# Decode attention with cached keys: in 13 of 16 heads the turned keys stream past the queries

## The chip, the cores and the metric

The kernel runs on one core of one Trainium2 chip. The metric is the device time of one execution in microseconds. TensorE is called PE here, VectorE DVE, ScalarE ACT, GpSimd POOL, and SyncE, which issues nearly all DMAs, SP.

## The reference

Eight sequences decode one token each (x is 8 x 1 x 448). The same attention block and the same mixer block are applied twice, in turn:

```python
x = x + _A_ref(_layernorm(x), A_k_cache, A_v_cache, A_wq, A_wo)
x = x + _B_ref(_layernorm(x), B_w1, B_w2, B_w3, B_w4)
x = x + _A_ref(_layernorm(x), A_k_cache, A_v_cache, A_wq, A_wo)
x = x + _B_ref(_layernorm(x), B_w1, B_w2, B_w3, B_w4)

def _A_ref(x, k_cache, v_cache, wq, wo):        # Hq 16, Hkv 8, Sk 4096, Dh 256
    q = (x @ wq).reshape(B, Sq, Hq, Dh).transpose(0, 2, 1, 3)
    k, v = repeat of the caches: two query heads share one key/value head
    scores = einsum("bhqd,bhkd->bhqk", q, k) * Dh ** -0.5
    return (softmax(scores) @ v).reshape(B, Sq, Hq * Dh) @ wo
```

With one token per sequence the token mixer of `_B_ref` sees only shifted, padded positions, so that the block is, in effect, a layernorm, a layernorm again, and a gelu MLP (448 to 1792 to 448) with its residual. Everything is bfloat16. Keys and values of one batch row and one key head are 2 MB each, and there are 64 such pairs. Since the caches are used by both attentions, they would be read twice; the kernel keeps a part of them in SBUF between the two.

## The kernel before, in words

**Units and slots.** A "head" here is one batch row and one key head, with its two query columns, in one of the two layers (attentions): 8 rows x 8 heads x 2 layers = 128. Its 4096 keys are loaded with 32 consecutive keys per partition, and are cut into four quarters (`u`) of eight key blocks (`s`) each. SBUF has 30 quarter slots of 4 KB per partition, shared by keys and values (`kv`). A load (`issue_kv`, L636) takes one to four quarters into neighbouring slots and waits on SP until the slots' last readers are done.

**One head's front (`front`, L1084).** For each quarter two pieces of 4 blocks are turned on PE: keys come as pairs of bfloat16 seen as one float32, so that a 128 x 128 float32 transpose turns 256 head dimensions at once (`transpose_piece`, L1401). Each piece fills one of four PSUM banks `psT`, and is copied back into its slot by DVE or ACT, whichever the planner picks (`evacuate`, L1332 and L1333). Even and odd head dimensions then lie interleaved along a slot's columns. The scores (`score`, L1119) use each turned block as the stationary operand, once for the even and once for the odd dimensions (`c`), and stream the two query columns, repeated 24 times (`REP`), past it: 64 matmuls of 48 columns per head. The 64 columns of scores lie in `psM` from column 64 (`SB`). They are copied to `sS` (L1177), reduced to a maximum (DVE, then POOL), and exponentiated on ACT into `pT` (L1194).

**One head's back (`back`).** P.V runs in four column strips of the array (32 matmuls of 256 columns, L1228), is copied out as two bfloat16 parts (`oS`, L1242 and L1244), summed over the strips (L1252), scaled (`oT`, L1258), and multiplied by the rows of wo (L1278) into a running row in `psR`. After the seventh head of a layer the row is turned back to columns by way of `oW` (L1291, L1293, L1060), and the eighth head is added.

**Order.** Key heads 0, 1 and 2 are "free" heads, loaded in both layers. Heads 3 to 6 keep their turned keys in SBUF from the first attention to the second; head 7 keeps one quarter, and leaves two quarters in the four `psT` banks and one half quarter in `kh`. Some values are kept too (`KEPT_V`). Per batch row the order is: first attention of the heads 3 to 7, with the free heads of the next row scored ahead; the MLP (`mid`, `mlp`), while the values of the next row's free heads pass; second attention in the order 6, 7, 5, 4, 3, 0, 1, 2. The second attention's queries are computed one head ahead (`second_queries`, L878 on PE, L1452 on DVE, into `q2T`). The results of the first six rows go through their last MLP together beside row 5.

A planner in the kernel (`Plan.schedule`) lays out all operations as a list schedule with written durations and priorities. It fixes each engine's order and each slot's tenant, lets "ev" operations go to DVE or ACT, and inserts filler matmuls (L1604) into PE's gaps. On the chip each engine goes through its list in that order and waits on semaphores.

Of the kernel before, what the change touches and what calls it, by code (L numbers as in the profile page):

```python
# [6 lines left out]
P = 128  # L7
B = 8
D = 448
HKV = 8  # L10
DH = 256
F = 1792
NC5 = 5
# [33 lines left out]
PV0 = 0  # L47
# [4 lines left out]
ST = 504  # L52
Q1 = 176


# [29 lines left out]
class Plan:  # L85
# [69 lines left out]
    def schedule(self):  # L155
# [78 lines left out]
        while n < len(self.ops):  # L234
# [128 lines left out]
            o.end = end  # L363
            if o.frees is not None:
                self.free_at[o.frees.slot] = end + self.LAT[e]
                self.tenant[o.frees.slot] = o
            for s in o.succ:
# [104 lines left out]
def bass_interleave_layers__gqa_block_cached__mixer_s_mlp__decode_kernel(  # L472
# [67 lines left out]
    rsy = sb("rsy", [P, 2, B], f32)  # L540
    q1b = [sb(f"q1b{i}", [P, 32], bf) for i in range(2)]
    lin = sb("lin", [P, 2, 2], f32)
    kh = sb("kh", [P, 1024], bf)
    q2T = [sb(f"q2T{i}", [P, 32], bf) for i in range(2)]
    cursor[0] = (cursor[0] + 31) // 32 * 32
# [13 lines left out]
    oW = over("oW", [P, 2, 2 * P], bf, hb)  # L559
    o_row = over("o_row", [B, D], bf, hb)  # L560
    cursor[0] = max(cursor[0], hb0 + 8 * P)
# [11 lines left out]

    sS = [sb(f"sS{i}", [P, 64], f32) for i in range(NS)]
    oS = sb("oS", [P, 2, DH], bf)
# [78 lines left out]
    YB = ["yb"]  # L654
    REG = ["hb", "g1", "hT", "t_h", "xc", "yb"]

    def const_a(gp):
        gp.memset(ident_f[:, :], 0.0)
        gp.memset(x_row[:, D:D + P], 0.0)
        gp.memset(mask[:, :], 1.0)  # L660
        gp.memset(x3T[:, :, :], 0.0)
        for t, one, minus in [(t, 1, 2) for t in x1c + x2c] + [(xf, 1, 0), (xf, 4, 5)]:
            gp.memset(t[:, :, one:one + 1], 1.0)
            last = gp.memset(t[:, :, minus:minus + 1], -1.0)
        return last
    plan.op("pool", const_a, 1.0, "const", wr=["ident0", "xr2", "mask0", "one", "x3all"])

# [150 lines left out]
    def norm(src, skey, second, B):  # L818
# [13 lines left out]
        mark(pe(mm, 36, rd=[skey, "one"], wr=[key], banks=[bk]))  # L832
        mo, xcv = mom[:, 0:2, 0:B], xc[:, :, 0:B]
        dv(lambda v: v.tensor_single_scalar(mo, ps[:, 0:2 * B].rearrange("p (c n) -> p c n", n=B),
# [7 lines left out]
        if second:  # L842
# [3 lines left out]
        dv(lambda v: v.tensor_tensor(xcv, src, bcast(mom[:, 0, 0:B], NC5, 1), ALU.add),  # L846
           rd=["mom", skey], wr=["xc", "g1"])
        dv(lambda v: v.tensor_tensor(xcv, xcv, bcast(mask[:, :], B, 2), ALU.mult), rd=["xc", "mask"],
           wr=["xc"])
        dv(lambda v: v.tensor_tensor(yb[:, :, 0:B], xcv, bcast(rsy[:, c - 1, 0:B], NC5, 1), ALU.mult),  # L850
           rd=["xc", "rsy"], wr=["yb", "g1"])
        if second:

            bs = base[:, :, 0:B]
            dv(lambda v: v.tensor_tensor(bs, xcv, bcast(rsy[:, 0, 0:B], NC5, 1), ALU.mult),
               rd=["xc", "rsy"], wr=["base"])
            dv(lambda v: v.tensor_tensor(bs, bs, src, ALU.add), rd=["base", skey], wr=["base"])
# [105 lines left out]
    def mlp(src, skey, n, dst, dkeys, rows_open=False):  # L963
# [5 lines left out]
        m = 14 * n  # L969
        h_, a_ = hb[:, 0:m], g1[:, 0:m]  # L970
        def scaled(r, y, keys):
# [28 lines left out]
        else:  # L1000
            norm(src, skey, True, n)
            pe(lambda t: h_mms(t, lambda kc: yb[:, kc, 0:n], ch, 0, n, n), 56,
               rd=YB + W3, wr=[kb], banks=[bk])
            dv(lambda v: v.tensor_copy(h_, ch[:, 0:m]), rd=[kb], wr=["hb"], banks=[bk])

        HB = ["hb"] + [("hb", r) for r in range(1, n) if few]
        dv(lambda v: v.scalar_tensor_tensor(a_, h_, GELU_C * GELU_K, h_, ALU.mult, ALU.mult),
           rd=HB, wr=["g1", "xc", "yb"])
        dv(lambda v: v.scalar_tensor_tensor(a_, a_, GELU_K, h_, ALU.add, ALU.mult),
           rd=HB + ["g1"], wr=["g1"])  # L1010
        plan.op("act", lambda a: a.activation(a_, a_, ACT.Tanh), 0.3, "chain",
                rd=["g1"], wr=["g1"], prio=urge[0] + len(plan.ops))
        if few and dst is not None:
# [5 lines left out]
               rd=["base", ("y", 0, B - 2), skey], wr=["base"])  # L1019
        dv(lambda v: v.scalar_tensor_tensor(hT[:, 0:m], a_, 1.0, h_, ALU.add, ALU.mult),  # L1020
           rd=HB + ["g1"], wr=["hT"])

# [4 lines left out]
        def y_mm(t, mts):  # L1027
            last = None
            for mt in mts:
                for fc in range(14):  # L1030
                    r = hT[:, fc * n:(fc + 1) * n]
                    if not few:
                        last = dup(t, ch, yc + mt * yw, yw, w4_sb, fc * D, mt, r, fc == 0, fc == 13)
                        continue
                    a = fc * D + (mt * P if mt < 4 else D - P)
                    if mt == 3 and fc == 13:
                        last = dup(t, ch, yc + mt * yw, yw, w4_sb, fc * D, mt, bcast(r, yw, 1), False, True)
                        continue
                    last = t.matmul(ch[:, yc + mt * yw:yc + (mt + 1) * yw], w4_sb[:, a:a + P], bcast(r, yw, 1),
                                    start=(fc == 0), stop=(fc == 13), skip_group_check=(mt == 3))  # L1040
            return last
        parts = Y_PARTS if few else [range(NC5)]
        for mts in parts:
            pe(lambda t, mts=mts: y_mm(t, mts), 14 * len(mts), rd=["hT"] + W4, wr=[kb], banks=[bk], width=yw)
        ps4 = ch[:, yc:yc + NC5 * yw].rearrange("p (a n) -> p a n", n=yw)[:, :, 0:n]
# [32 lines left out]
    def first_q(b, prio):  # L1078
        for c in range(2):
            dv(lambda v, c=c: v.tensor_copy(  # L1080
                q1b[b % 2][:, :].rearrange("p (h c j) -> p h c j", c=2, j=2)[:, :, c, :],
                psM[:, Q1 + b:Q1 + 32 * B:B].rearrange("p (h j c) -> p h c j", j=2, c=2)[:, :, c, :]),
               rd=["q1"], wr=[("q1b", b % 2, c)], banks=[M], prio=prio)

    def front(layer, b, h, prio=None):
# [8 lines left out]
        if layer == 0:  # L1094
            def rhs(c):
                return q1b[b % 2][:, 4 * h + 2 * c:4 * h + 2 * c + 2]
            qk = [("q1b", b % 2, 0), ("q1b", b % 2, 1)]
        else:
            def rhs(c):
                return q2T[b % 2][:, 4 * h + 2 * c:4 * h + 2 * c + 2]  # L1100
            qk = [("q2", b, h)]
        ks = dict(kept_k)
# [21 lines left out]
        def score_op(u, ss, where_of, keys):  # L1124
# [3 lines left out]
                           rd=qk + keys, wr=[("sc", par, x) for x in range(u, 4)], banks=[bk],  # L1128
                           prio=prio and prio + len(plan.ops))
        for u in range(4):  # L1130
            full = [("s", ks[u], 0), ("s", ks[u], 1)]
# [14 lines left out]
            if last_head and u == 1:  # L1146
                if layer == 0:
                    score_op(u, range(4), of_kh, ["kh"])
                    o = score_op(u, range(4, 8), of, [("s", ks[u], 1, 0), ("s", ks[u], 1, 1)])
                    o.frees = ks[u]  # L1150
                else:
# [3 lines left out]
                continue  # L1155
            if layer and last_head and u in (2, 3):
                pass
            o = score_op(u, range(8), of, full)
            if layer and h == first2[b] and u == 3:
# [9 lines left out]
            if layer and u == 3 and h == first2[b]:  # L1169
                lent[b] = ks[u]  # L1170
            elif u not in keep_k:
                o.frees = ks[u]
        hi = len(plan.ops) - 10 ** 5
# [30 lines left out]
    def back(layer, b, h):  # L1204

        kept_k, vs, held, nr = state.pop((layer, b, h))
        free_p.append(nr)
        keep_v = KEPT_V.get(h, ()) if layer == 0 else ()
# [12 lines left out]
        for u in range(4):  # L1221

            def pv(t, u=u, q=vs[u]):
                last = None
                for s in range(8):
                    i = 8 * u + s
                    g4 = 32 * (i % 4)
                    last = t.matmul(ps[g4:g4 + 2, PV0:PV0 + DH], pT[nr][:, i, :],  # L1228
                                    slot_ap(q, s * 256, 256), start=(i < 4), stop=(i >= 28),
# [8 lines left out]
            if u not in keep_v:  # L1238
                o.frees = vs[u]

# [84 lines left out]
    tcount = [0]  # L1325
    held_banks = set()

    def evacuate(i, pc, bank):
# [84 lines left out]
    def result(n, at):  # L1413
# [3 lines left out]
        def ot(t):  # L1417
            last = None
            for kc in range(4):
# [5 lines left out]
        mark(dv(lambda v: v.tensor_copy(o_row[0:n, :], ps[0:n, :].bitcast(bf)[:, 0:D]), dur=0.5,  # L1425
           rd=[key], wr=["o_row"] + REG, banks=[bk]))
        plan.op("sp", lambda eng: eng.dma_start(out[at:at + n, 0, :], o_row[0:n, :]), 0.1, "out",
                rd=["o_row"] + REG, wr=[("done", n)],
                dma=(s_out, 16), prio=loads[0] + OUT_AT)
# [17 lines left out]
    def second_queries(b, h, prio):  # L1447
# [4 lines left out]
        dv(lambda v: v.scalar_tensor_tensor(  # L1452
            q[:, 4 * h:4 * h + 4].rearrange("p (c j) -> p c j", c=2),
            cs_q[:, 4 * h:4 * h + 4].rearrange("p (c j) -> p c j", c=2), mom2[b % 2][:, 2:3],
            psM[:, SC:SC + 4].rearrange("p (j c) -> p c j", c=2), ALU.mult, ALU.add),
           rd=["psM", ("mom2", b), "cs_q"], wr=[("q2", b, h)], banks=[M], prio=prio)

# [206 lines left out]
```

## Time and profile before

| what | value |
|---|---|
| median of three runs | 1105.56 us (1102.48, 1105.56, 1107.56) |
| span of the profiled execution | 1108.6 us, 42701 instructions |
| mean granted clock of TensorE | 0.918 |
| PE busy, matmuls | 964.7 us, 19483 |
| DVE busy, ACT busy | 587.9 us, 291.6 us |
| HBM read | 434.18 MB, 392 GB/s over the span |
| packets of q1, share of 16 DMA engines | 61268, 96.6% |

The span is that of the one profiled execution, from its first to its last instruction. No time of its own is reported for that execution beside the span; the span is 1.0 us above the slowest of the three runs and 3.0 us above their median. "busy" counts instructions as the profiler shows them; a matmul's row holds its way through the pipeline too, so that the mean of one (285 ns for a transpose) is longer than the distance from one to the next. "issue" as a releaser means that an engine waited for nothing that the profile shows.

### The profile page before, as it was taken

To read this page: it belongs to the slowest core of one execution; us is meant where nothing else is said; L and a number is where in the kernel's file an instruction comes from. 1 tells how busy PE (TensorE), PEld (TensorE's weight loads), DVE (VectorE), ACT (ScalarE), POOL (GpSimd) and SP (SyncE) were. 2 spreads that over 40 slices of the span, in tenths; PEclk is the share of its full clock that TensorE was granted. 3 is DMA by queue.
4 is the path that set the end of the run, shared out by engine and by line. 5 is a ranking of instruction groups with operands and counts; after the bars stand their busy time and mean duration, and the time that the engine had idled before them with its cause. 6 is when DMAs were issued, how large, how long until landed. Compare 5 with 4: busy or idle time off the path is not lost.

```text
span 1108.6 us, 42701 instructions
## 1 busy us (share of the span) xinstructions
PE 964.7 (87%) x19483; PEld 772.7 (70%) x19483; DVE 587.9 (53%) x1869; ACT 291.6 (26%) x862; POOL 98.2 (9%) x277
## 2 busy tenths in 40 slices
PE   4889889898899888898989988899889998888885
PEld 4678657785678756697668855788567885786673
DVE  4245445565465553565546554566546665455644
ACT  1133112340234311243124411244023330233230
POOL 0000010110100001010000101011010100110010
PEclk9899989997999888999799988999789998999796
DMA  9999999999999999999999999999999999999892
GB/s 334 409 425 417 380 406 425 422 419 388 397 423 426 399 388 406 410 399 407 377 425 425 421 394 400 425 422 416 388 398 426 422 372 377 397 420 383 292 415 91
DMA packets 61456, 436.95 MB, mean 394 GB/s; under 512 B 6606, under 2 KB 9820, under 8 KB 40924
## 3 DMA queue, kind: packets, MB, share of 16 engines
q1 hardware_dynamic: 61268, 434.22, 96.6%
q8 instruction: 153, 2.51, 0.9%
q14 instruction: 27, 0.22, 0.0%
q10 hardware_dynamic: 8, 0.00, 0.0%
HBM read 434.18 MB, written 0.01 MB: 392 GB/s over the span
## 4 chain that ended last, share of the span: by engine, by line
PE 58%; DMA 25%; SPq 5%; DVE 5%; issue 4%; ACT 2%; POOL 1%; DVEq 0%
PE psT L1401 22%; PE psM L1119 16%; DMA kv<-in_A_v_cache_dram 13%; DMA kv<-in_A_k_cache_dram 11%; PE psP L1228 10%; SPq L636 4%; PE psR L1278 4%; PE psM L878 2%; SPq L619 1%; ACT pT L1194 1%; PE psP L1252 1%; DVE oS L1244 1%; DVE oS L1242 1%; DMA w_sb<-in_B_w_dram 1%; PE psM L1060 1%
## 5 line engine op out<-in xcount | busy, mean ns | idle before, releaser
L1401 PE MATMUL psT<-ident_f,kv 128*128 128x128 f32 x2752 | 384.4, 285 | 14.7 <-DMA kv<-in_A_k_cache_dram 14.0
L1332 DVE COPY kv<-psT 128x512 f32<-128x512 f32 x411 | 282.5, 691 | 158.8 <-PE psT L1401 155.5
L1401 PEld LDWEIGHTS psT<-ident_f,kv 128*128 128x128 f32 x2752 | 307.8, 145 | 38.4 <-issue 18.9
L1333 ACT COPY kv<-psT 128x512 f32<-128x512 f32 x309 | 180.6, 587 | 456.9 <-PE psT L1401 368.1
L1228 PE MATMUL psP<-kv,pT 128*2 128x256 bf16 x4096 | 190.6, 295 | 39.0 <-issue 21.2
L1119 PEld LDWEIGHTS psM<-q2T,kv 128*128 128x128 bf16 x3968 | 124.6, 100 | 48.0 <-issue 36.5
L1119 PE MATMUL psM<-q2T,kv 128*128 128x48 bf16 x3968 | 139.4, 188 | 17.1 <-issue 15.7
L1119 PEld LDWEIGHTS psM<-q1b,kv 128*128 128x128 bf16 x4032 | 131.4, 97 | 19.2 <-issue 8.5
L1119 PE MATMUL psM<-q1b,kv 128*128 128x48 bf16 x4032 | 140.0, 184 | 4.9 <-ACT pT L1194 2.6
L1228 PEld LDWEIGHTS psP<-kv,pT 128*2 128x2 bf16 x4096 | 76.5, 83 | 79.6 <-issue 33.9
L1184 POOL PARTITION_ALL_REDUCE gm<-pm x128 | 45.6, 357 | 767.0 <-DVE pm L1182 694.9
L1194 ACT ACTIVATE pT<-sS,nb,fac 128x32 bf16<-128x32 f32 x128 | 52.9, 419 | 158.7 <-DVE nb L1188 158.7
L1177 DVE COPY sS<-psM 128x64 f32<-128x64 f32 x128 | 28.6, 224 | 117.3 <-PE psM L1119 114.9
L1242 DVE CAST oS<-psP 128x256 bf16<-128x256 f32 x128 | 54.0, 422 | 68.0 <-PE psP L1228 66.6
L1278 PE MATMUL psR<-wo_sb,oT 128*1 128x448 bf16 x444 | 68.8, 396 | 3.5 <-DVE oT L1258 2.3
L1198 POOL PARTITION_ALL_REDUCE Db<-rs x128 | 51.3, 400 | 208.4 <-ACT pT L1194 208.4
L1194 ACT ACTIVATE pT<-sS,nb 128x32 bf16<-128x32 f32 x128 | 40.9, 327 | 72.1 <-DVE nb L1188 72.1
L1252 PEld LDWEIGHTS psP<-sel,oS 128*128 128x128 bf16 x512 | 25.4, 100 | 49.1 <-DVE oS L1244 42.9
L1252 PE MATMUL psP<-sel,oS 128*128 128x2 bf16 x512 | 32.3, 167 | 31.3 <-DVE oS L1244 29.3
L1244 DVE TENSOR_TENSOR oS<-psP,oS 128x256 bf16<-128x256 f32 x128 | 54.2, 423 | 3.4
L878 PEld LDWEIGHTS psM<-x2c,wq_sb 128*128 128x128 bf16 x768 | 30.8, 99 | 16.6 <-DVE pm L1182 6.6
L1258 DVE TENSOR_TENSOR oT<-psP,rc 128x4 bf16<-128x4 f32 x128 | 20.3, 159 | 37.2 <-PE psP L1252 34.3
(187 smaller groups left out, 652.4 us busy)
## 6 DMA issues: line engine op xcount, KB each, us to landing
kv<-in_A_k_cache_dram SPq DMA_DIRECT2D x66, 2048.0 KB, 18.8
kv<-in_A_v_cache_dram SPq DMA_DIRECT2D x53, 2048.0 KB, 16.0
kv<-in_A_v_cache_dram SPq DMA_DIRECT2D x196, 512.0 KB, 8.1
kv<-in_A_k_cache_dram SPq DMA_DIRECT2D x43, 512.0 KB, 8.1
kv<-in_A_k_cache_dram SPq DMA_DIRECT2D x13, 1536.0 KB, 15.1
kv<-in_A_v_cache_dram SPq DMA_DIRECT2D x15, 1024.0 KB, 9.5
kv<-in_A_v_cache_dram SPq DMA_DIRECT2D x6, 1536.0 KB, 10.7
wo_sb<-in_A_wo_dram SPq DMA_DIRECT2D x1, 3584.0 KB, 45.6
```

Of the source, the lines that this page charges most:

```text
L878: last = t.matmul(bank[:, at + i * step:at + i * step + copies], w, r, start=(kc == 0), stop=(kc == 3))
L1119: last = t.matmul(ps[:, SB + 2 * i:SB + 2 * i + 2 * REP], a()[:, c:256:2], bcast(rhs(c), REP, 1), start=(c == 0), stop=(c == 1))
L1194: return a.activation(pT[nr][:, :, :].rearrange("p i j -> p j i")[:, jj, :], sview[:, jj, :], ACT.Exp, bias=nb[nm][:, jj:jj + 1], scale=sc ...
L1198: plan.op("pool", lambda gp: gp.partition_all_reduce(Db[nr][:, :], rs[nr][:, :], P, RO.add), 0.5, "sum", rd=[("rs", nr, 0), ("rs", nr, 1)] ...
L1228: last = t.matmul(ps[g4:g4 + 2, PV0:PV0 + DH], pT[nr][:, i, :], slot_ap(q, s * 256, 256), start=(i < 4), stop=(i >= 28), skip_group_check= ...
L1242: plan.op("dve", lambda v: v.tensor_copy(oS[:, 0, :], po), 0.36, "o", rd=[("pv", par, x) for x in range(4)], wr=["oS0"], banks=[bk], prio=hi)
L1244: plan.op("dve", lambda v: v.tensor_tensor(oS[:, 1, :], po, oS[:, 0, :], ALU.subtract), 0.36, "o", rd=["oS0"] + [("pv", par, x) for x in r ...
L1252: last = t.matmul(ps[:, PV1 + 2 * c:PV1 + 2 * c + 2], oS[:, w, c:DH:2], sel[:, :], start=(w == 0), stop=(w == 1))
L1278: last = t.matmul(psR[r:r + 1, 0:D], oT[no][:, i % 2, i // 2:i // 2 + 1], wo_sb[:, a:a + D], start=(k == 1 and i < 2), stop=(k == turn_at ...
L1332: return e.tensor_copy(dst, psT[bank][:, :])
L1333: return e.copy(dst, psT[bank][:, :])
L1401: last = t.transpose(psT[bank][:, s * P:(s + 1) * P], src, ident_f[:, :])
```

## The change

In every head but three kinds the two halves of the scores are computed the other way around. The exceptions are key head 7 in both layers, and the head that comes first in the second attention (head 6); 13 of the 16 heads of a batch row are changed.

- The queries become the stationary operand: `q1b` and `q2T` hold the queries of all eight heads, 16 columns for even and 16 for odd dimensions, and 16 columns of zero behind them (48 in all). Columns 16c to 16c+32 are loaded.
- `score_rows`: for half a head (two quarters) the turned keys stream past, 512 columns at a time, in four column strips of the array and for both `c`: eight matmuls into one `psT` bank. Each strip of 32 partitions then holds score rows of all heads for a quarter of those keys; only the two rows of this head are wanted.
- `turn_rows`: DVE or ACT copies that bank to `sr` as bfloat16, and four matmuls with `sr` as the stationary operand and eight identity columns that pick this head's rows bring the scores into `psM` as columns again. `sr` lies where `hb`, `g1`, `hT` and `oW` lie.
- Scores reach `sS` as bfloat16, in another order of blocks, which P.V undoes by its index `k`.
- The two quarters of a half are now freed together, behind the row matmuls. In the second layer the rows read `q2T` of all heads, so that the next head's query is written after them.
- The MLP of the first six rows moves its buffers from the region of `hb` to that of `kh`.

```diff
-    q1b = [sb(f"q1b{i}", [P, 32], bf) for i in range(2)]
+    q1b = [sb(f"q1b{i}", [P, 48], bf) for i in range(2)]
...
+    sr = over("sr", [P, 512], bf, hb)
...
-    sS = [sb(f"sS{i}", [P, 64], f32) for i in range(NS)]
+    sS = [sb(f"sS{i}", [P, 64], bf) for i in range(NS)]
...
+        for q in q1b + q2T:
+            gp.memset(q[:, :], 0.0)
...
+        rows = ROWS and not last_head and not (layer and h == first2[b])
+        by_rows[layer, b, h] = rows
+        if rows and layer:
+            qk = [("q2", b % 2, x) for x in range(HKV)]
...
+            if rows:
+                if u % 2 == 0:
+                    continue
+                o = score_rows([ks[u - 1], ks[u]], qall, qk + full + [("s", ks[u - 1], 0), ("s", ks[u - 1], 1)], prio)
+                turn_rows(u // 2, h, o.tbank, par, prio)
+            else:
+                o = score_op(u, range(8), of, full)
...
+            elif rows:
+                o.frees = [ks[x] for x in (u - 1, u) if x not in keep_k]
...
+                    k = 16 * (u // 2) + 4 * (s % 4) + 2 * (u % 2) + s // 4 if in_rows else i
-                    last = t.matmul(ps[g4:g4 + 2, PV0:PV0 + DH], pT[nr][:, i, :],
+                    last = t.matmul(ps[g4:g4 + 2, PV0:PV0 + DH], pT[nr][:, k, :],
...
+    def score_rows(qs, qall, keys, prio):
+        bank = next_bank()
+        def mm(t):
+            last = None
+            for c in range(2):
+                for g in range(4):
+                    last = t.matmul(psT[bank][32 * g:32 * g + 32, :], qall[:, 16 * c:16 * c + 32],
+                                    slot_ap(qs[g // 2], g % 2 * 1024, 1024)[:, c:1024:2], start=(c == 0),
+                                    stop=(c == 1), skip_group_check=True, tile_position=(0, 32 * g))
+            return last
+        o = plan.op("pe", mm, (0.47, 0.92, 1024, 8), "scr", rd=keys, wr=[("psT", bank)],
+                    banks=[("T", bank)], prio=prio and prio + len(plan.ops))
+        o.tbank = bank
+        return o
+    def turn_rows(half, h, bank, par, prio):
+        def ev(e):
+            if e is nc.vector:
+                return e.tensor_copy(sr[:, :], psT[bank][:, :])
+            return e.copy(sr[:, :], psT[bank][:, :])
+        plan.op("ev", ev, {"dve": 0.71, "act": 0.6}, "evr", rd=[("psT", bank)], wr=SR, banks=[("T", bank)],
+                prio=prio and prio + len(plan.ops)).tbank = bank
+        picks = ident_b.rearrange("p (g c) -> p g c", g=4)[:, :, 2 * h:2 * h + 2]
+        def mm(t):
+            last = None
+            for k in range(4):
+                a = SB + 32 * half + 8 * k
+                last = t.matmul(psM[:, a:a + 8], sr[:, k * P:(k + 1) * P], picks, start=True, stop=True)
+            return last
+        plan.op("pe", mm, (0.17, 0.17, 32, 4), "scturn", rd=SR + ["ident_f"],
+                wr=[("sc", par, x) for x in range(2 * half, 4)], banks=[M], prio=prio and prio + len(plan.ops))
```

## The prediction, made blind

> **What bounds the kernel now.** I read the page first: the engine shares, the slices and the DMA queues.
>
> ```profile
> PE 964.7 (87%) x19483; PEld 772.7 (70%) x19483; DVE 587.9 (53%) x1869; ACT 291.6 (26%) x862; POOL 98.2 (9%) x277
> DMA  9999999999999999999999999999999999999892
> GB/s 334 409 425 417 380 406 425 422 419 388 397 423 426 399 388 406 410 399 407 377 425 425 421 394 400 425 422 416 388 398 426 422 372 377 397 420 383 292 415 91
> q1 hardware_dynamic: 61268, 434.22, 96.6%
> q8 instruction: 153, 2.51, 0.9%
> ```
>
> The best slices move some 427 GB/s, and 434.22 MB at that rate is 1017 us. So 92 of the 1108.6 us can be had at all: the start, about 22 us behind the last landing (DMA moves nothing from 1088 on), and dips that return about every 131 us, once per batch row. TensorE is nearly full beside it. Next the groups, for prices (busy us, mean ns of one, then the idle before):
>
> ```profile
> L1119 PE MATMUL psM<-q2T,kv 128*128 128x48 bf16 x3968 | 139.4, 188 | 17.1 <-issue 15.7
> L1119 PE MATMUL psM<-q1b,kv 128*128 128x48 bf16 x4032 | 140.0, 184 | 4.9 <-ACT pT L1194 2.6
> L1228 PE MATMUL psP<-kv,pT 128*2 128x256 bf16 x4096 | 190.6, 295 | 39.0 <-issue 21.2
> L1332 DVE COPY kv<-psT 128x512 f32<-128x512 f32 x411 | 282.5, 691 | 158.8 <-PE psT L1401 155.5
> L1333 ACT COPY kv<-psT 128x512 f32<-128x512 f32 x309 | 180.6, 587 | 456.9 <-PE psT L1401 368.1
> ```
>
> With the groups that read kh (5.8 and 2.9 us), scores cost 288.1 us for 8192 matmuls: 35.2 ns each, 2.25 us per head. Then the table of windows, cut at a steady stretch and at the dips (PE, PEld, DVE, ACT, POOL busy; clock; DMA share; GB/s):
>
> ```profile
> 720.00:730.00 10.00, 8.96 (x158) 6.85 (x157) 6.46 (x20) 4.25 (x10) 0.76 (x2) 1.00 1.01 424
> 548.00:554.00 6.00, 5.75 (x188) 4.43 (x176) 2.54 (x11) 1.82 (x8) 1.34 (x4) 1.00 0.87 283
> 940.00:948.00 8.00, 7.65 (x256) 6.20 (x251) 3.56 (x15) 1.82 (x8) 1.51 (x4) 1.00 0.89 288
> 900.00:910.00 10.00, 10.00 (x185) 8.82 (x181) 6.42 (x19) 4.55 (x14) 1.51 (x4) 1.00 0.95 345
> ```
>
> In the steady stretch DMA is full and TensorE keeps up. In the dips at 548 and 940, where the kept keys of the second attention are scored, DMA runs dry while TensorE is full: 31 matmuls per us. SP's own waits say why: the slots come free with scores.
>
> ```profile
> SPq L636 <- PE psM L1119: 426.5, 102, 26.2
> SPq L636 <- PE psP L1228: 390.6, 160, 20.9
> ```
>
> Last the timeline of PE near the end:
>
> ```profile
> 1065.88 0.61 PE L1228 MATMUL psP<-kv,pT 128*2 128x256 bf16 x16
> 1066.42 0.25 PE L878 MATMUL psM<-x2c,wq_sb 128*128 128x24 bf16 x3
> ...
> 1070.88 0.66 PE L1119 MATMUL psM<-q2T,kv 128*128 128x48 bf16 x13 [2.35 <-issue]
> ...
> 1085.31 0.59 PE L1228 MATMUL psP<-kv,pT 128*2 128x256 bf16 x6 [2.86 <-issue]
> ```
>
> After dense stretches PE stands for 2 to 3 us on "issue", which is no semaphore. Queue q8 brings 153 packets of 16.4 KB while PE runs 38966 instructions, 255 to a packet, so I read these as waits for code. From 1050 to 1080, gaps included, PE got through 637 matmuls: 128 in 6.0 us.
>
> **The change, part by part.** It touches 104 heads (13 of 16, eight rows).
>
> Taken away: 64 score matmuls per head. In the timeline 48 of them run from 1059.95 to 1061.16 at full clock, 25.2 ns each, so 1.61 us per head; by the mean, 2.25.
>
> Added on PE, per half head: eight matmuls of 512 columns in four column strips, then four of 8 columns. Nearest to the first is L1228, which also goes in four strips: 16 take 0.54 us (fence above), and 32 take 0.98 (1055.94 to 1056.92), so 27.5 ns for 256 columns and 0.10 us per group. For 512 columns I take 55 ns: a group of eight is 0.54 us. Ends: 53 ns (two of the 26 ns seen at best) and 293 (12.6 us over 43 fillers of 512 columns run singly). The strips of L1228 plainly overlap, so I stay at the low end; twice its mean of 46.5, so 93 ns, is my bound. The stride of two in the streamed keys should cost nothing: the fillers stream identity columns at that stride, and their 256-column form takes 275 ns median against 272 for the unstrided L1228. The four turning matmuls resemble L1252, four of which take 0.12 us (1052.63 to 1052.75); ends 0.10 and 0.25 (63 ns by its mean). Per head: 2 x (0.54 + 0.12) = 1.32 us against 1.61 at full clock; by means 2 x (0.74 + 0.25) = 1.98 against 2.25. So 0.27 to 0.29 us saved per head, some 30 us of PE time, and up to 0.9 where rows run well and columns at the mean. The Trainium skill, page "TensorEngine Tiling (Array Packing)", section "Key Properties", says that switching the tiling mode drains the array. By that rule each strip group pays a fixed price; the measured 0.10 us agrees and is already in the sum.
>
> Matmul count: 24 instead of 64 per head, 4160 fewer of 19483, about 33 code packets fewer. At 6.0 us per 128, 40 matmuls are 1.9 us per head where code is what is short. A kept head has some 120 matmuls (64 scores, 32 for P.V, 4 and 4 for sum and output, 16 for the next query): three in a row ask for 17 us of code, while their values (3 x 2.1 MB at 427 GB/s) need 14.8. With 80 they ask for 11.3, below the DMA.
>
> Added on DVE and ACT: 208 copies of 128x512, 691 or 587 ns, 122 to 144 us over two engines now busy 880 of 2217. Writing bf16 should cost what writing f32 does, since DVE's 128x256 cast takes 422 ns, in line with 691 for twice as much; ends 587 and 844. The narrower sS copy I hold at 224 ns (ends 166, a small cast, and 422). In the steady window DVE has 3.5 of 10 us free, ACT 5.7, and a head needs 1.3 more.
>
> Waits added. (1) A turning matmul waits for its copy, and all of PE's queue stands behind it; the cover is transposes or P.V (0.98 us). Without it: 0.69 + 0.25 = 0.94 us. (2) One sr buffer: the second half's copy waits for the first half's turn, and the copies share that space with hb and oW. A head's scores are ready 1 to 1.5 us later. The cover is the head of lag before P.V, 4.9 us of values. (3) q2T of the next head waits until the rows have read the old ones; DVE's evacuations queue behind it, and the next rows wait for it. About 0.5 us, covered by P.V; uncovered 24 kept heads x 0.5 = 12 us. (4) Two slots come free together, the first about 1.07 us later (two transpose groups at 0.53). SP's next load, and every V load queued behind it, moves with it. A 2 MB key load lands after 18.8 us, of which 4.9 is its own, so 14 us of queue cover it; in a dip there is no cover, and 8 x 1 us is the price. Against that, paired slots make 4-quarter loads likelier. (5) Four memsets on POOL delay the identity by about 0.2 us (20 instructions took 1.03), hidden behind the first loads. (6) Ten instead of eight uses of four psT banks per fresh head: two engines empty a bank per 0.32 us, 3.2 of a head's 9.8 us.
>
> Sum. The dips after the second queries, against 427 GB/s, lose 1.5 us (284 to 290), 1.1 (416), 2.0 (548), 1.0 (678), 1.0 (808), 2.6 (940): 9.2. Heads 6 and 7 keep the old path there, so I credit half: 4.6. The steady holes at 482, 888 and 900 lose 4.6 in all; the saved PE time is small there: 1.5. The tail: from 1088 to 1095.9 PE works off P.V at clocks of 0.57 and 0.85, late by the 2.86 us stall at 1082.45; six heads less 40 matmuls (11 us of code) remove it, and some of the cold clock: 3.4. Together 9.5. Against it 1.5 for longer score chains where nothing covers them. Net 8.0: 1100.6 for the profiled span. The span stands 3.0 above the median shown (1105.56), so 1097.5.
>
> **The rivals.** First, no change: the dips are set by heads 6 and 7, which keep columns, by the MLP chain before them and by short loads; and stalls at full DMA cost nothing (at 420 to 430 PE stood 5 us on issue while DMA moved 419 GB/s). Then only part of the tail comes, 2 us: 1103.5. Beside it stands the rule of the Trainium skill, page "Runtime: NRT & Kernel Launch", section "Instruction fetch mechanics", that code blocks stream in behind execution and crossing one is mostly hidden. By that rule fewer instructions gain nothing in themselves. The trace speaks against it with its gaps of 2 to 3 us, about 44 us of issue in all, though few of them meet an empty DMA queue. As a mechanism of this kernel it is the same 2 us: PE time in the tail, and no code relief. Half of the chance of 0.22 for this result is for either reason.
>
> Second, slower: PE stands at the turning matmuls. It decides once a head's uncovered wait passes the 0.29 us saved at full clock. The place is the kept heads, where transposes are absent: 24 heads x 2 x 0.94 = 45 us of PE, less 24 x 0.93 (2.25 - 1.32) = 22, leaves 23; the queue absorbs half, as it does with the issue gaps: +11.5, so 1117. For it: that stretch is where DMA is already dry, and orders are fixed in advance. Against: ACT is idle 8 of 10 us there, and P.V stands ready. 0.30. That the scores stay on the old path is excluded by the code.
>
> **How the numbers follow.** Forecast 0.48, around 1097.5, own range 1085 (all dips, the steady holes and 6 us of tail) to 1101; 0.01 of it lies within 0.5% of 1105.56. The whole range is 1085 to 1119: the top takes in the slower case with 2 us over it. A measurement of this kernel tells about 0.5%, 5.5 us, from no change (the three runs span 5.1). Faster by over that: 0.47; within: 0.23; slower: 0.30.
>
> **What would show it.** Right: PE's count near 15300, q8 near 120 packets, row groups of eight at 0.5 to 0.6 us; issue before PE below 20 us; GB/s in the dips above 350; less than 20 us from the last landing to the end. Wrong: DVE sr or PE psM with an idle wait on the sr copies of over 20 us; row matmuls near 93 ns or more; dips as deep as now, or DMA short in steady stretches.

## The result, and the profile after

The changed kernel takes 1095.51 us (median of five runs, 1089.77 to 1097.29) against 1105.56 us, which stays the median of before with five runs: the ratio is 0.9903, with a 95% interval of 0.9879 to 0.9927. The profiled execution of the changed kernel spans 1094.1 us. It is 14.5 us shorter than the one of before, where the medians differ by 10.0. For this one, and for the profiled executions of the experiments, a time is reported beside the span, 1.8 to 2.5 us above it; by that the profiled execution of before took some 1110 us, an estimate, which is above all five runs. So what single spans divide up below is read as shares.

The page of the changed kernel, in the lines that answer to those of before:

```profile
PE 948.4 (87%) x15414; PEld 636.6 (58%) x15414; DVE 665.9 (61%) x2004; ACT 335.0 (31%) x935; POOL 98.0 (9%) x281
DMA  9999999999999999999999999999999999999892
GB/s 333 409 424 421 391 403 425 426 418 375 410 424 427 412 390 392 425 424 415 372 425 425 424 404 390 425 425 420 398 380 427 424 417 381 396 426 410 310 412 120
q1 hardware_dynamic: 60260, 434.22, 97.5%
q8 instruction: 121, 1.98, 0.7%
```

TensorE runs 4069 matmuls fewer and DVE and ACT some 78 and 43 us more; the code queue brings 121 packets instead of 153. The chain of work that ended last shows best what happened. It is the first line of the page's fourth part, of the kernel before and then of the changed one:

```profile
PE 58%; DMA 25%; SPq 5%; DVE 5%; issue 4%; ACT 2%; POOL 1%; DVEq 0%
```

```profile
DMA 57%; PE 31%; DVE 6%; ACT 2%; issue 2%; SPq 1%; POOL 0%; POOLq 0%; DVEq 0%
```

The end hung on TensorE; now it hangs on the transfers. The groups of the changed kernel (busy us, mean ns of one, idle before it):

```profile
L1387 DVE CAST sr<-psT 128x512 bf16<-128x512 f32 x157 | 108.4, 691 | 73.6 <-PE psT L1374 60.2
...
L1374 PE MATMUL psT<-kv,q1b 128*32 128x512 bf16 x896 | 72.5, 394 | 17.9 <-ACT kv L1408 14.9
...
L1374 PE MATMUL psT<-kv,q2T 128*32 128x512 bf16 x768 | 60.3, 397 | 3.4 <-DVE kv L1407 2.0
...
L1398 PE MATMUL psM<-ident_f,sr 128*128 128x8 bf16 x832 | 52.4, 170 | 7.9 <-DVE sr L1387 6.5
...
L1388 ACT CAST sr<-psT 128x512 bf16<-128x512 f32 x51 | 29.8, 585 | 42.2 <-PE psT L1374 37.9
```

A group of eight row matmuls costs 132.8 / 208 = 0.64 us on average, and four turning matmuls 0.25. A head takes 1.78 us where 64 old matmuls took 2.25. The copies cost 138 us. TensorE's turning matmuls wait 6.5 us for DVE's copies in all, since something else stands ready nearly every time.

The windows that answer to those of before, each at its place in the new run (two dips, a steady stretch, and one that answers to 900 to 910; columns as before):

```profile
412.00:420.00 8.00, 7.55 (x175) 4.51 (x175) 4.58 (x17) 0.96 (x5) 0.97 (x4) 1.00 0.93 319
...
932.00:938.00 6.00, 5.83 (x146) 3.57 (x143) 4.09 (x14) 0.91 (x4) 0.75 (x2) 1.00 0.91 310
710.00:720.00 10.00, 8.34 (x126) 5.54 (x126) 6.49 (x20) 2.66 (x7) 0.75 (x2) 1.00 1.00 423
896.00:906.00 10.00, 8.33 (x157) 6.51 (x155) 6.86 (x19) 2.84 (x8) 0.82 (x3) 1.00 1.02 413
```

These two dips are still there, at 310 to 319 GB/s where the deepest of before were at 283 to 288; of the others one has filled (284 to 290, from 318 to 406 GB/s) and another is as deep (800 to 808, at 310). What has gone is the hole in a steady stretch: the window of before at 900 to 910 had TensorE busy for 10.00 of 10 us and 345 GB/s; here TensorE has 1.7 us to spare and DMA moves 413. SP's waits have moved with the work, from scores to P.V and row matmuls:

```profile
SPq L643 <- PE psP L1257: 517.7, 150, 22.6
SPq L643 <- PE psT L1374: 174.8, 53, 17.6
SPq L643 <- PE psM L1136: 74.9, 44, 4.7
```

Last the timeline of PE through the kept heads of the second attention, in row 3. First the kernel before: head 6 begins its scores, two long waits on issue follow, and the first fresh keys are turned.

```profile
540.36 0.82 PE L1119 MATMUL psM<-q2T,kv 128*128 128x48 bf16 x16
...
558.23 0.26 PE L1119 MATMUL psM<-q2T,kv 128*128 128x48 bf16 x4 [2.45 <-issue]
...
564.44 0.46 PE L1119 MATMUL psM<-q2T,kv 128*128 128x48 bf16 x12 [0.69 <-issue]
...
566.80 1.09 PE L1401 MATMUL psT<-ident_f,kv 128*128 128x128 f32 x8
```

Then the changed kernel, from head 6 through the rows of heads 5, 4 and 3:

```profile
534.68 0.80 PE L1136 MATMUL psM<-q2T,kv 128*128 128x48 bf16 x16
...
544.31 1.08 PE L1374 MATMUL psT<-kv,q2T 128*32 128x512 bf16 x16
...
549.38 1.09 PE L1374 MATMUL psT<-kv,q2T 128*32 128x512 bf16 x16
...
551.76 0.66 PE L1476 MATMUL psT<-ident_f,kv 128*128 128x128 f32 x4
...
554.53 1.12 PE L1374 MATMUL psT<-kv,q2T 128*32 128x512 bf16 x16
```

From head 6's first score to the first fresh key turned it was 26.4 us, and it is 17.1. Over the first six rows the same distance is 25.3 to 29.2 us before, mean 26.9, and 15.9 to 19.6 after, mean 17.7. The three kept heads hold back the landed keys less: now TensorE waits for keys more often, as the list of waits says for the kernel before and the changed one.

```profile
PE psT L1401 <- DMA kv<-in_A_k_cache_dram: 14.0, 12, 2.5
```

```profile
PE psT L1476 <- DMA kv<-in_A_k_cache_dram: 25.0, 32, 2.8
```

Not all of the shorter distance is shorter scores. The planner has also laid a new order: in row 3 five groups of matmuls for next queries (L878) stand in between before, and three (L892) after. The experiments come back to this.

### The profile page after: what moved, and what is told of

Read it like the earlier page. It is cut to its first block, busy times and chain, and to the rows that moved or that the text cites. A ratio compares the mean times of both kernels' runs of the same rounds, so it can differ in the third digit from the quotient of the medians.

```text
span 1094.1 us, 34653 instructions
## 1 busy us (share of the span) xinstructions
PE 948.4 (87%) x15414; PEld 636.6 (58%) x15414; DVE 665.9 (61%) x2004; ACT 335.0 (31%) x935; POOL 98.0 (9%) x281
## 4 chain that ended last, share of the span: by engine, by line
DMA 57%; PE 31%; DVE 6%; ACT 2%; issue 2%; SPq 1%; POOL 0%; POOLq 0%; DVEq 0%
DMA kv<-in_A_v_cache_dram 39%; DMA kv<-in_A_k_cache_dram 15%; PE psT L1476 8%; PE psP L1257 8%; PE psT L1374 4%; PE psM L1136 3%; PE psR L1307 2%; PE psM L892 2%; DMA wqx_sb<-in_A_wq_dram 2%; DMA w_sb<-in_B_w_dram 1%; PE psM L1054 1%; DVE kv L1407 1%; ACT pT L1221 1%; SPq L626 1%; ACT kv L1408 1%
## 5 line engine op out<-in xcount | busy, mean ns | idle before, releaser
L1476 PEld LDWEIGHTS psT<-ident_f,kv 128*128 128x128 f32 x2752 | 296.7, 142 | 111.8 <-issue 69.6
L1407 DVE COPY kv<-psT 128x512 f32<-128x512 f32 x388 | 265.7, 690 | 135.3 <-PE psT L1476 131.4
L1387 DVE CAST sr<-psT 128x512 bf16<-128x512 f32 x157 | 108.4, 691 | 73.6 <-PE psT L1374 60.2
L1374 PE MATMUL psT<-kv,q1b 128*32 128x512 bf16 x896 | 72.5, 394 | 17.9 <-ACT kv L1408 14.9
L1221 ACT ACTIVATE pT<-sS,nb,fac 128x32 bf16<-128x32 bf16 x128 | 52.6, 417 | 106.9 <-DVE nb L1215 106.9
L1307 PE MATMUL psR<-wo_sb,oT 128*1 128x448 bf16 x444 | 67.4, 387 | 3.5 <-DVE oT L1287 3.1
L1374 PE MATMUL psT<-kv,q2T 128*32 128x512 bf16 x768 | 60.3, 397 | 3.4 <-DVE kv L1407 2.0
L1398 PEld LDWEIGHTS psM<-ident_f,sr 128*128 128x128 bf16 x832 | 42.5, 97 | 30.7 <-DVE sr L1387 16.5
L1398 PE MATMUL psM<-ident_f,sr 128*128 128x8 bf16 x832 | 52.4, 170 | 7.9 <-DVE sr L1387 6.5
L1221 ACT ACTIVATE pT<-sS,nb 128x32 bf16<-128x32 bf16 x128 | 40.8, 326 | 57.7 <-DVE nb L1215 57.6
L1281 PEld LDWEIGHTS psP<-sel,oS 128*128 128x128 bf16 x512 | 24.4, 99 | 39.5 <-DVE oS L1273 29.2
L1204 DVE CAST sS<-psM 128x64 bf16<-128x64 f32 x128 | 27.8, 217 | 29.5 <-PE psM L1136 20.2
L1388 ACT CAST sr<-psT 128x512 bf16<-128x512 f32 x51 | 29.8, 585 | 42.2 <-PE psT L1374 37.9
```

The source lines that it names most:

```text
L1221: return a.activation(pT[nr][:, :, :].rearrange("p i j -> p j i")[:, jj, :], sview[:, jj, :], ACT.Exp, bias=nb[nm][:, jj:jj + 1], scale=sc ...
L1281: last = t.matmul(ps[:, PV1 + 2 * c:PV1 + 2 * c + 2], oS[:, w, c:DH:2], sel[:, :], start=(w == 0), stop=(w == 1))
L1307: last = t.matmul(psR[r:r + 1, 0:D], oT[no][:, i % 2, i // 2:i // 2 + 1], wo_sb[:, a:a + D], start=(k == 1 and i < 2), stop=(k == turn_at ...
L1374: last = t.matmul(psT[bank][32 * g:32 * g + 32, :], qall[:, 16 * c:16 * c + 32], slot_ap(qs[g // 2], g % 2 * 1024, 1024)[:, c:1024:2], sta ...
L1387: return e.tensor_copy(sr[:, :], psT[bank][:, :])
L1398: last = t.matmul(psM[:, a:a + 8], sr[:, k * P:(k + 1) * P], picks, start=True, stop=True)
```

## The experiments

Ratios are to the kernel before, run beside each experiment on the same chip, with 95% intervals. The first four leave the planned order and the slots as they are and change only what an operation issues. In most of the others the planner lays a new order, so that a few us between two of them can be the order's own.

**Matmul count and TensorE time put back.** Two kernels give each row group of the changed kernel about the same extra TensorE time, once as code and once not.

```diff
+            for _ in range(20):
+                t.matmul(psT[bank][:, 0:2], ident_b, ident_b[:, 0:2], start=True, stop=True)
             for c in range(2):
                 for g in range(4):
```

> The changed kernel, its order and slots untouched, with 20 extra two-column matmuls (results overwritten) ahead of each group of row matmuls: the 40 matmuls per head that the change saved are back as code, and with them some 1.0 us of TensorE time per changed head (25 ns each). Theory C (code: the number of matmuls is what was short): the gain goes, 1102 to 1106. Theory T (TensorE time in the steady stretches is what was short): the gain goes too, and as 1.0 us is more than the 0.29 us saved at full clock, 1104 to 1112. Rival D (DMA paces, TensorE has room): under 1098.

```diff
+            for n in (512, 512, 128):
+                t.matmul(psT[bank][:, 0:n], ident_b, bcast(ident_b[:, 0:n // 4], 4, 1), start=True, stop=True)
             for c in range(2):
                 for g in range(4):
```

> The changed kernel with three wide extra matmuls (512, 512 and 128 columns, results overwritten) ahead of each group of row matmuls instead: the same 1.0 us of TensorE time per changed head, but only 6 matmuls of code instead of 40. Theory C: little is lost, 1096 to 1099, clearly under the one with 40 small matmuls. Theory T: like that one, 1104 to 1112. Rival D: under 1098.

The 40 small ones gave 1168.22 us, 1.0571 (1.0536 to 1.0606), the wide ones 1155.61 us, 1.0464 (1.0439 to 1.0489). Both are far above every expectation. In the timelines 20 small matmuls take 0.59 us (502.65 to 503.24) and three wide ones 0.62 (501.75 to 502.37), so a changed head got 1.2 us, 123 to 129 us over all; 73 and 60 us of it came through to the end. Added TensorE time therefore counts, and above all in the steady stretches: by the split of losses further down, some 45 of the 60 us lie there. The changed kernel stands where DMA and TensorE take about the same. The small ones cost 12.6 us more, though by the timelines they take no more TensorE time. They are 34 more matmuls per head, 27.6 packets of code at 256 instructions, so at most 0.46 us per packet. It is a bound and no price, since the clock differs too: the mean granted clock of the profiled executions was 0.937 with the small ones and 0.946 with the wide ones, and in each of the six runs with small ones it lies below that of every run with wide ones. By these figures TensorE lost 0.063 x 1163 = 73 us to the clock against 0.054 x 1155 = 62, an estimate that alone makes 11 of the 12.6 us.

**Longer copies.**

```diff
-            if e is nc.vector:
-                return e.tensor_copy(sr[:, :], psT[bank][:, :])
-            return e.copy(sr[:, :], psT[bank][:, :])
+            for a in (0, 64):
+                if e is nc.vector:
+                    last = e.tensor_copy(sr[a:a + 64, :], psT[bank][a:a + 64, :])
+                else:
+                    last = e.copy(sr[a:a + 64, :], psT[bank][a:a + 64, :])
+            return last
```

> The changed kernel with each copy of score rows made in two halves of 64 partitions one after the other: about 0.69 us (DVE) or 0.59 us (ACT) more in every chain from row matmuls to turning matmuls, 208 times, and as much more load on those engines. If PE or the next maximum stands at these copies (the slower rival of the prediction), the time grows by 10 us or more, at most 208 x 0.69 = 143. If they are covered, it stays within 3 us of the changed kernel, 1093 to 1099.

It took 1141.46 us, 1.0338 (1.0310 to 1.0365): 46 us for 208 longer copies, so they are not covered. TensorE's waits for the copies, by the list of waits:

```profile
PE psM L1401 <- DVE sr L1388: 74.2, 142, 1.3
...
PE psM L1401 <- ACT sr L1390: 14.6, 43, 0.9
```

In the changed kernel DVE's line was 6.5 us in 15 waits. The cover of the turning matmuls is the planner's order, made for 0.71 and 0.60 us; copies that take twice as long as planned made TensorE stand 185 times.

**Relief without rows.** The kernel before with 24 score matmuls per head where the change has 24.

```diff
                 for u, s, a in parts:
                     i = 8 * u + s
+                    if few and s % 8 > 2:
+                        continue
```

> The kernel before, its order and slots untouched, with only 24 of the 64 score matmuls in the 104 heads that the change touches (5 of 8 key blocks of each quarter are left out of the scores). It relieves TensorE by 40 matmuls and 1.0 us per head without copies, row matmuls, paired slots or a new order. If relief of TensorE is the cause: 1092 to 1097, at or below the changed kernel. If the gain came from the paired slots, the longer loads or the new order of the planner: 1103 to 1107.

1097.72 us, 0.9929 (0.9903 to 0.9954). Relief of TensorE in the old order gives most of the gain. TensorE's busy sum falls by 66.1 us, nearly twice what the rows save (35 without the fillers, see below), no copies are paid for, and still it gives no more. One reason is DMA: it has 56% of this kernel's chain, and TensorE waits for keys far longer than before.

```profile
PE psT L1404 <- DMA kv<-in_A_k_cache_dram: 70.7, 39, 6.3
```

Another can be the clock: the mean granted clock is 0.872 here against 0.918 before, and below 0.88 in all twelve runs, so that a part of the relief went into slower matmuls. That DMA alone sets a limit of 8 to 10 us is therefore likely, and not shown. The distance to the first fresh key is 21.0 us on average here.

**Side changes.**

```diff
-ROWS = True
+ROWS = False
```

> The changed kernel with the row scores switched off in all heads: the old scores, but with what else the change brought (zeroed, wider query tiles in the new column order, sS as bf16, the buffers of the first six rows' last MLP in the region of kh). If the rows alone make the gain: 1103 to 1108. If the side changes matter: 1095 to 1101.

1104.53 us, 0.9994 (0.9966 to 1.0021): the side changes do nothing that shows.

**Where: by layer.**

```diff
-        rows = ROWS and not last_head and not (layer and h == first2[b])
+        rows = ROWS and not layer and not last_head and not (layer and h == first2[b])
```

> Rows only in the first attention: 7 heads per batch row, 56 in all, all with freshly loaded keys. The prediction put most of the gain in the second attention's kept heads and the tail, which stay old here: 1102 to 1105 by it. If the gain lies in the steady stretches, where fresh keys are turned and scored, this has about half of it or more: 1098 to 1101.

```diff
-        rows = ROWS and not last_head and not (layer and h == first2[b])
+        rows = ROWS and layer and not last_head and not (layer and h == first2[b])
```

> Rows only in the second attention: heads 5, 4, 3 with kept keys and 0, 1, 2 with fresh ones, 48 heads. By the prediction's terms (dips after the second queries and the tail) nearly all of the gain is here: 1096 to 1099. If the steady stretches make it, half or less: 1099 to 1103.

The first attention alone gave 1105.62 us, 1.0008 (0.9990 to 1.0026): nothing, with 56 of the 104 heads. The second alone gave 1097.79 us, 0.9925 (0.9897 to 0.9954), as the prediction's terms asked.

**Where: within the second attention.** First the heads whose keys are kept, then those with fresh keys.

```diff
-        rows = ROWS and not last_head and not (layer and h == first2[b])
+        rows = ROWS and not last_head and not (layer and h == first2[b]) and layer and h in kept_heads
```

> Rows only in the three kept heads (5, 4, 3) of the second attention, 24 heads in all: there no keys are turned, code runs short, and slots come free with the scores. If the gain of the second attention (7.7 us with rows in six heads) is made there, as the prediction's dips say: 1098 to 1101. If it is made by the fresh heads 0, 1, 2: 1103 to 1106.

```diff
-        rows = ROWS and not last_head and not (layer and h == first2[b])
+        rows = ROWS and not last_head and not (layer and h == first2[b]) and layer and h in free_heads
```

> Rows only in the heads 0, 1, 2 of the second attention, 24 heads, whose keys are loaded fresh and turned. If the gain of the second attention comes behind the kept heads, where TensorE catches up: 1098 to 1101. If it is made by the kept heads: 1103 to 1106.

The three kept heads alone, 24 of 104 heads, gave 1097.07 us, 0.9930 (0.9902 to 0.9958). The fresh heads alone gave 1102.43 us, 0.9972 (0.9951 to 0.9993), which is little and only just clear of nothing. The distance from head 6's first score to the first fresh key goes along with it: 16.4 us with rows in the kept heads alone, 16.7 in the whole second attention, 26.1 in the first attention alone, 26.4 in the fresh heads alone, 26.2 with the rows off.

The distance mixes two causes, though. With the relief alone, in the old order, it is 21.0 us. With the new order, and more TensorE time per head than the rows saved put back (the two kernels with added matmuls), it is 21.7 and 20.1 us, still some 5 us under the 26.9 of before. So both the relief and the new order that the rows allow make it shorter, and no run has that order without the rows. That relief alone gives most of the time is shown for a relief nearly twice as large; how the changed kernel's own 10 us divide between relief and order is not.

**Paired slots.**

```diff
-ROWS = True
+ROWS = False
...
-            elif rows:
-                o.frees = [ks[x] for x in (u - 1, u) if x not in keep_k]
+            elif not last_head and not (layer and h == first2[b]):
+                if u % 2:
+                    o.frees = [ks[x] for x in (u - 1, u) if x not in keep_k]
             elif u not in keep_k:
```

> The changed kernel with the row scores off, and the slots of two quarters freed together behind the second one's old scores, as the rows free them. If pairing the slots gives longer loads and so part of the gain: 1098 to 1103. If it only holds a slot longer: 1105 to 1109, at or above the kernel with the rows off.

With the rows off, 1100.83 us, 0.9960 (0.9941 to 0.9978), 3.7 us below the kernel with the rows off and single slots. The intervals of the two touch, so this is likely, not settled. Together with rows in the second attention (the same freeing, and the condition of the second attention alone instead of `ROWS = False`):

```diff
-        rows = ROWS and not last_head and not (layer and h == first2[b])
+        rows = ROWS and not last_head and not (layer and h == first2[b]) and layer
```

> Rows in the second attention (six heads per batch row), old scores in the first, but there too the slots of two quarters are freed together. Rows in the second attention alone gave 1097.8; paired slots without any rows gave 1100.8 against 1104.5 with the rows off. If the two gains add: 1092 to 1095, at or below the changed kernel with 56 heads fewer in rows. If DMA now sets the pace and nothing adds: 1096 to 1099.

1095.07 us, 0.9913 (0.9882 to 0.9943). It does as well as the changed kernel with 56 fewer heads in rows, but no better that can be told, and not clearly better than rows in the second attention alone (0.9925): whether the two gains add stays open.

**Copies on ScalarE.**

```diff
-        plan.op("ev", ev, {"dve": 0.71, "act": 0.6}, "evr", rd=[("psT", bank)], wr=SR, banks=[("T", bank)],
+        plan.op("act", ev, 0.6, "evr", rd=[("psT", bank)], wr=SR, banks=[("T", bank)],
```

> The changed kernel with all 208 copies of score rows on ScalarE (157 were on VectorE). Making each copy 0.6 us longer cost 46 us, so they have no slack. If it is VectorE's load that makes them late: 1088 to 1093, under the changed kernel. If it is the time of the copy itself, fixed in the planned order: 1093 to 1098. If ScalarE's exponentials get in the way: over 1098.

1098.99 us, 0.9949 (0.9923 to 0.9975): no gain from freeing VectorE of 157 copies, and probably a loss against the changed kernel's 0.9903 (the intervals just touch). ACT in the way of its exponentials was the rival that named this side; that it is the cause was not shown.

## Why the prediction was right, step by step

**The total** came out: 1097.5 forecast, 1095.51 measured, within its own range of 1085 to 1101. That it came so near is in part luck: the term for the steady holes was too small, the 1.5 us against did not show, and the paired slots and the planner's new order, which may both have helped, are not in the sum.

**The operations** were sized right. Row groups: 0.54 to 0.74 us forecast, 0.57 in a steady stretch (702.32 to 702.89 in the changed kernel) and 0.64 on average. Turning: 0.12 forecast with ends of 0.10 and 0.25, measured 0.25 by the mean, so at its upper end. Copies: 122 to 144 us, measured 138. PE time saved: some 30 us; the busy sum fell by 16.3 while filler matmuls grew by 18.4 (43 and 146 of them to 56 and 224), so 35 without them. The matmul count, 15414 against 15300, missed by the extra fillers.

**Where the gain arises** was right, and the kept-heads kernel shows it: three heads per row give 7.2 of 10 us, with the planner's order for them.

**Where it appears** was wrong. I split 9.5 us into dips 4.6, steady holes 1.5 and tail 3.4. Loss against 427 GB/s, with 50 us around each row's MLP counted as the stage with the dip, went from 45.7 to 40.3 us there, from 13.1 to 7.6 in the steady rest, and from 19.9 to 17.9 behind the last landing. So in this pair the steady holes were the mis-sized term: about 5.5 us instead of 1.5. My reason there was the saving per head, 0.29 us, which is small. The kernel with the rows off, which gained nothing, also lost 13.2 us in the steady rest, so that this fall does not look like chance; behind the last landing it lost 17.2, so that the 2.0 us of the tail, forecast as 3.4, can't be told from chance. The sign "less than 20 us from the last landing to the end" says nothing either, since the kernel before already stood at about 20 and not at the 22 that I gave.

It would be simple to say that the time won at the kept heads is carried on, as TensorE reaches the fresh keys 9 us earlier. The kernel with rows in the kept heads alone speaks against that as the whole reason: its first fresh key is as early (16.4 us), but by the same split it loses 39.3, 11.3 and 13.9 us. Its gain lies around the MLPs and behind the last landing, much as I had split mine, and least in the steady rest. So the steady gain of 5.5 us needs rows in more heads than these; why it then adds so little to the total is open. All of these are single executions.

The two dips shown stayed (the sign "above 350 GB/s" failed). The 1.5 us against, for longer chains, did not show as a loss.

**Code** was half right. PE's idle time on issue fell from 43.9 to 4.3 us, as the sign of under 20 asked. But 6.0 us per 128 matmuls was the pace of a dense stretch (TensorE was busy for 26.07 of the 30 us from 1050 to 1080), not the price of a packet: in the pair of kernels with added matmuls a packet cost at most 0.46 us. The one with small matmuls brings 153 packets, as many as the kernel before, and its TensorE stands on issue for only 6.6 us; so the number of packets alone does not make these waits, and that they are for code is still a reading. The bound stands nearer to the rule of the Trainium skill that I weighed against the trace (page "Runtime: NRT & Kernel Launch", section "Instruction fetch mechanics": crossing a block is mostly hidden). How much of the kept heads' gain is code and how much TensorE time was not separated there; it stays open.

**The slower rival** named a real price, and the forecast put its cover right: PE waited 6.5 us for DVE's copies, not 45. The rival's saving of 22 us set rows at full clock (1.32 us) against columns at their mean (2.25); mean against mean, as measured, it is 0.47 us per head and 11 us. The longer copies show how near this case lay; 0.6 to 0.7 us more per copy cost more than four times the gain. A wait that I did not list is the larger one: the row matmuls stand for the last turned keys to be copied back, 15.0 us for ACT and 3.3 for DVE.

**Paired slots** I priced as a loss of up to 8 us in the dips, and then left out of the sum against likelier long loads. The run with paired slots and old scores points to a gain of about 3.7 us instead. The first attention's rows, on the other hand, which also pair their slots, gave nothing at all. Why is open: its 112 copies, its paired slots and the planner's new order are all in that one run, and none was taken alone in the first attention.

## What to carry to other kernels

Where two resources are nearly balanced, relief can pay mainly at the one stage in which the scarce one falls behind: 24 heads gave 7.2 us where 104 gave 10. Ask of each added copy in a fixed order how long it was planned to take, since its cover was laid out for that. A price per instruction that is read off a stretch in which TensorE is full need not hold elsewhere. Where a change makes a planner lay a new order, try the relief in the old order as well, and look at the granted clock beside each time.

## What was not expected of the hardware

The weight loader stands idle behind row groups. Before the transposes' weights it waited on issue for 69.6 us in 172 waits, against 18.9 in 63 in the kernel before:

```profile
PEld psT L1476 <- issue: 69.6, 172, 0.8
```

```profile
PEld psT L1401 <- issue: 18.9, 63, 0.4
```

Of the 172, 112 waits with 49.9 us come directly behind a row group, which is 0.45 us each and most of a row group's 0.57; 34 more come behind the products with wo (L1307) and 25 behind P.V. The timeline of the weight loader shows one such wait:

```profile
702.32 0.12 PEld L1374 LDWEIGHTS psT<-kv,q2T 128*32 128x32 bf16 x8 [0.17 <-issue]
702.89 0.42 PEld L1476 LDWEIGHTS psT<-ident_f,kv 128*128 128x128 f32 x4 [0.44 <-issue]
```

All eight sets of row weights are in after 0.12 us, and the next full-width weights begin only at 702.89, when the row group has streamed. In the changed kernel the transposes' weights were thus not loaded while a strip group in front of them streamed.
